# Twenty columns of a V page instead of ten are parked in PSUM between two layers, and one weight piece changes places with a K page

## The chip, the cores and the metric

The kernel runs on one core of one Trainium2 chip. The metric is the device time of one execution in microseconds (us); lower is better.

## The reference

A decoder for one token, two layers with the same weights and the same K and V caches. Cut to what matters:

```python
def _A_ref(x, k_cache, v_cache, wq, wo):          # attention over the last W = 4096 positions
    q = (x @ wq).reshape(1, 1, 32, 192)           # 32 heads of 192
    scores = einsum(q, k_window) * 192 ** -0.5
    o = einsum(softmax(scores), v_window)
    return o.reshape(1, 1, 32 * 192) @ wo

x = x + _A_ref(_layernorm(x), k_cache, v_cache, wq, wo)
x = x + silu_glu(_layernorm(x), w1, w3, w2)       # 640 -> 1536 -> 640
# ... and both lines once more: layer 1 reads the same caches and weights again
```

K and V of the window are 2 x 32 x 4096 x 192 bf16 values, 100.7 MB, read once per layer. Whatever is still on the chip from layer 0 need not be read again in layer 1.

## The kernel before

The heads are worked on in four blocks of eight, each in four "pages" (z = 0 to 3) of K and of V. A page is 64 columns of 192 bf16 values on 128 partitions, 3.1 MB. Nearly all of SBUF is one tile `pg` with seven page slots. All loads go through one plan in a fixed order, and are issued by SP. A load can be issued when everything that was in its place has been read:

```python
def plan(key, at, n, src):
    queue.append((key, at, n, src))

def need(key):
    while key not in place:
        k, at, n, src = queue.pop(0)
        ...
        nc.sync.dma_start(out=pg[:, at:at + n], in_=src)
        place[k] = live[k] = (at, n)
    ...
```

Layer 1 goes through the blocks backwards (3, 2, 1, 0). So the K and V pages of block 3, last used in layer 0, stay in the seven slots over the layer boundary. One V page (block 3, z 0) has no slot. 54 of its 64 columns lie in a separate area, and the other ten wait in PSUM, where DVE puts them with two transposes as 32-bit words and from where it takes them back with two more. The separate area also keeps 12 columns of the page of block 2, z 3:

```python
KEPT_T = 54          # columns of V page (3, 0) kept in SBUF
KEPT_2 = 12          # columns of V page (2, 3) kept in SBUF
PSUM_T = 10          # columns of V page (3, 0) kept in PSUM
...
half = PSUM_T // 2 * DH
held = [t[:, 0:half // 2].bitcast(U32) for t in (aside, s_two[0])]     # two PSUM banks

def hold(x):                                       # end of layer 0
    for i in range(2):
        nc.vector.transpose(held[i], words(x[:, -2 * half:], i))

def put_back():                                    # layer 1, after the first softmax
    key, at = vkeys[1, 3, 0][0], slot(2)
    place[key] = live[key] = (at, 2 * half)
    for i in range(2):
        nc.vector.transpose(words(pg[:, at:at + 2 * half], i), held[i])
```

In layer 1 the page (2, 3) needs only the columns that were not kept:

```python
if (b, z) == (2, 3):
    plan_v(1, b, z, (slot(vs[z]), TP - KEPT_2), (None, KEPT_2))        # 64 - 12 = 52 loaded
```

At the boundary all seven slots are taken. Until layer 1 has used up its first kept K page, only small pieces can be loaded, into rings in the work area: wo, w1, w3, w2 and the wq pieces of layer 1. wq comes in three groups: group 0 (five chunks of 384 KB, columns for block 3), group 1 (five of 768 KB) and group 2 (five of 384 KB). The plan there is:

```python
for g, (c2, n) in enumerate(QGROUPS):
    if g == 2:
        plan_k(1, 2, 0, 1)            # first new K page, into slot 1
    for c in range(NCH):
        o = 4 * QC * c + QC * c2
        plan(("wq", 1, g, c), RING["q"][g][c], QC * n, wq_v[:, o:o + QC * n])
```

`chunks("b3")` in the kernel means group 1, chunk 3; I use the same names: b0 to b4 are group 1, c0 to c4 group 2.

PSUM has eight banks: three fixed tiles (two score tiles and `aside`), three work buffers (`ps_a`) and two small ones (`ps_m`). The Trainium skill, "PSUM — Partial Sum Buffer", section "Specifications (TRN2)", gives 8 banks of 2 KiB per partition. Five columns of 192 bf16 values are 1,920 B, so a bank holds five of them and ten columns fill two banks.

## Time and profile before

| | before |
|---|---|
| median of the first 6 executions | 528.36 us (526.78 to 528.73) |
| span in the profile | 526.9 us (an execution of 528.68 us) |
| bytes over the DMA engines | 219.27 MB, 416 GB/s on average |
| PE / DVE busy | 54% / 48% |
| rate from 20 to 250 us and from 330 to 510 us | 430 and 428 GB/s |
| rate from 270 to 310 us (layer boundary) | 364 to 402 GB/s |

The lines of the page that say so (busy time and share of each engine; then the bytes):

```profile
span 526.9 us, 6780 instructions
PE 282.1 (54%) x2978; PEld 120.1 (23%) x2978; DVE 253.0 (48%) x309; ACT 41.6 (8%) x93; POOL 17.3 (3%) x62
DMA packets 16311, 219.27 MB, mean 416 GB/s; under 512 B 1945, under 2 KB 1945, under 8 KB 7961
```

The table by stretches of time follows: for each stretch (in us from the start) its length, the busy time of each engine, the granted TensorE clock, the busy share of the DMA engines and what they moved.

```profile
core 0: us, PE busy (x) PEld busy (x) DVE busy (x) ACT busy (x) POOL busy (x), PEclk, DMA share, GB/s
20.00:250.00 230.00, 115.79 (x1040) 43.87 (x1036) 129.49 (x125) 15.63 (x36) 0.00 (x0) 0.77 1.01 430
...
270.00:280.00 10.00, 6.23 (x92) 4.11 (x92) 2.10 (x9) 0.79 (x3) 0.00 (x0) 0.50 0.99 381
280.00:290.00 10.00, 6.68 (x109) 5.31 (x102) 1.28 (x6) 0.78 (x3) 2.25 (x7) 0.50 1.01 402
290.00:300.00 10.00, 6.41 (x120) 3.52 (x122) 3.24 (x13) 0.88 (x3) 0.72 (x3) 0.50 1.02 369
300.00:310.00 10.00, 7.70 (x85) 2.99 (x81) 1.34 (x1) 0.48 (x1) 0.00 (x0) 0.84 1.00 364
310.00:320.00 10.00, 6.67 (x108) 2.15 (x101) 2.89 (x12) 1.76 (x4) 2.30 (x6) 0.84 1.01 417
...
330.00:510.00 180.00, 105.11 (x1076) 43.34 (x1072) 97.72 (x100) 12.17 (x28) 0.50 (x2) 0.74 1.00 428
```

The last two columns are the ones to read. In all these stretches the DMA engines are busy all the time (share 0.99 to 1.02). But between 270 and 310 us they move 364 to 402 GB/s and otherwise about 430. So a busy share of 1.00 does not mean full rate.

The issues at the boundary, from the timeline of SP (start, duration, what, how many; neighbours are merged, so the row at 303.48 covers c0 to c4):

```profile
286.43 15.42 SPq L111 DMA_DIRECT2D pg<-in_A_wq_dram  x10
302.88 0.55 SPq L111 DMA_DIRECT2D pg<-in_A_k_cache_dram  x1
303.48 6.11 SPq L111 DMA_DIRECT2D pg<-in_A_wq_dram  x5
309.64 2.86 SPq L111 DMA_DIRECT2D pg<-in_A_k_cache_dram  x2
```

The first new K page is issued at 302.88 us, when PE has read the first kept K page, and c0 right after it. c0's ring place had been read about 8 us earlier. SP issues in order, so the K page holds c0 back.

The transposes into and out of PSUM on DVE, with the idle time before an instruction and what ended it in brackets:

```profile
250.04 0.69 DVE L279 STREAM_TRANSPOSE aside<-pg 128x480 uint32<-128x480 uint32 x1
250.63 0.65 DVE L279 STREAM_TRANSPOSE s_ps_176<-pg 128x480 uint32<-128x480 uint32 x1
...
327.17 0.86 DVE L285 STREAM_TRANSPOSE pg<-aside 128x480 uint32<-128x480 uint32 x1
327.96 0.64 DVE L285 STREAM_TRANSPOSE pg<-s_ps_176 128x480 uint32<-128x480 uint32 x1
330.96 0.17 DVE L425 RECIPROCAL rl<-rl_ps 128x1 f32<-128x1 f32 x1 [2.37 <-PE rl_ps L423]
```

A transpose takes 0.64 to 0.86 us. After the way back DVE waits 2.37 us for the row sums from PE: this is slack. How long SP waited for the second transpose of the way in, from the queue's own waits (total us, times, longest):

```profile
SPq L111 <- DVE s_ps_176 L279: 7.8, 1, 7.8
```

SP waits at this point, but the two V pages that it issued before are still being loaded: their first matmuls wait for data until 257.34 and 264.66 us.

Last, a row of the chain of waits (start, length, what). The chain passes through DVE for 24.7 us after the boundary:

```profile
331.13 24.74 DVE pg L345 x15
```

### The profile page before, as it was taken

The page shows a single profiled execution, that of the slowest core. Times are in us where ns is not written, and L with a number is a line of the kernel's source. Part 1 is how long each engine was busy: PE and PEld are TensorE (multiplying, and loading weights), DVE is VectorE, ACT ScalarE, POOL GpSimd, SP SyncE. Part 2 cuts the span into 40 slices and gives each one's busy share as a digit, 9 for nine tenths or more (in the row PEclk, how much of TensorE's full clock was granted, in tenths as well). Part 3 has the DMA queues.
Part 4 walks back from the last instruction along what each step waited for, and adds up shares of the span by engine and source line. Part 5 has one row for each costly group of instructions (what it writes and reads, how often), then busy time and mean ns, then how long its engine had stood idle before and what let it go on. Part 6 is the DMA issues. An engine that isn't in the chain of part 4 may idle for free.

```text
span 526.9 us, 6780 instructions
## 1 busy us (share of the span) xinstructions
PE 282.1 (54%) x2978; PEld 120.1 (23%) x2978; DVE 253.0 (48%) x309; ACT 41.6 (8%) x93; POOL 17.3 (3%) x62
## 2 busy tenths in 40 slices
PE   1417755550755507647456773694774335844464
PEld 0201111110311103213125321221321121212153
DVE  1269974436394174753001226898475366453010
ACT  0000020000200011002000006001100020002000
POOL 6000000000000000000001004000000000000000
PEclk9997887776589757777555595888687757977555
DMA  8999999999999999999999999999999999999994
GB/s 358 422 442 423 436 422 438 423 435 431 428 430 428 433 425 435 428 421 436 420 403 390 370 374 443 428 431 427 428 430 430 433 429 431 428 428 426 419 409 168
DMA packets 16311, 219.27 MB, mean 416 GB/s; under 512 B 1945, under 2 KB 1945, under 8 KB 7961
## 3 DMA queue, kind: packets, MB, share of 16 engines
q1 hardware_dynamic: 16136, 218.83, 98.3%
q8 instruction: 23, 0.38, 0.3%
q14 instruction: 8, 0.06, 0.0%
q10 hardware_dynamic: 144, 0.00, 0.0%
HBM read 218.83 MB, written 0.00 MB: 415 GB/s over the span
## 4 chain that ended last, share of the span: by engine, by line
DMA 60%; DVE 17%; PE 12%; issue 7%; ACT 3%; SPq 0%; ACTq 0%; DVEq 0%
DMA pg<-in_A_k_cache_dram 39%; DVE pg L345 13%; DMA pg<-in_B_w_dram 7%; DMA pg<-in_A_v_cache_dram 7%; PE s_ps_177 L353 5%; DMA pg<-in_A_wq_dram 5%; PE y_ps L448 2%; PE o_ps L416 2%; PE s_ps_176 L353 2%; DMA xb<-in_A_x_dram 2%; ACT pg L404 2%; ACT pg L391 1%; DVE pg L394 1%; DVE pg L337 1%; DVE otd L440 0%
## 5 line engine op out<-in xcount | busy, mean ns | idle before, releaser
L345 DVE STREAM_TRANSPOSE pg<-pg 128x1536 uint32<-128x1536 uint32 x112 | 188.5, 1743 | 94.2 <-DMA pg<-in_A_k_cache_dram 94.2
L353 PE MATMUL s_ps_176<-pg 128*32 128x512 bf16 x384 | 87.2, 617 | 53.8 <-DVE pg L345 53.8
L353 PE MATMUL s_ps_177<-pg 128*32 128x512 bf16 x288 | 65.7, 616 | 52.1 <-DVE pg L345 49.6
L416 PE MATMUL o_ps<-pg 128*16 128x384 bf16 (+1 forms) x1024 | 74.7, 377 | 27.3 <-DMA pg<-in_A_v_cache_dram 18.9
L353 PEld LDWEIGHTS <-pg 128*32 128x32 bf16 x672 | 41.1, 116 | 202.8 <-issue 190.0
L416 PEld LDWEIGHTS <-pg 128*16 128x16 bf16 (+1 forms) x1024 | 30.8, 98 | 59.2 <-issue 40.1
L433 PE MATMUL ot_ps<-o_sb,pg 128*128 128x192 bf16 x16 | 3.8, 342 | 62.0 <-ACT o_sb L430 62.0
L448 PE MATMUL y_ps<-otd,pg 128*128 128x1 bf16 x540 | 23.3, 178 | 11.4 <-DVE otd L440 6.7
L448 PEld LDWEIGHTS <-pg 128*128 128x128 bf16 x540 | 23.1, 131 | 13.5 <-issue 8.0
L391 ACT ACTIVATE pg<-s_ps_176,pg 32x512 bf16<-32x512 f32 x8 | 6.6, 822 | 185.7 <-DVE pg L388 185.6
L437 DVE SCALAR_TENSOR_TENSOR om<-ot_ps,rl,dsel 128x192 f32<-128x192 f32 x8 | 3.1, 388 | 37.2 <-PE ot_ps L433 37.2
L391 ACT ACTIVATE pg<-s_ps_177,pg 32x512 bf16<-32x512 f32 (+1 forms) x8 | 6.6, 823 | 166.0 <-DVE pg L388 157.5
L404 ACT COPY pg<-pg 32x256 bf16<-32x256 bf16 (+1 forms) x36 | 17.7, 491 | 6.8 <-DVE pg L394 6.2
L394 DVE STREAM_TRANSPOSE pg<-pg 128x1024 bf16<-128x1024 bf16 x8 | 10.0, 1245 | 15.6 <-ACT pg L391 15.6
L232 POOL MEMSET pg<- 128x128 f32 (+1 forms) x6 | 1.4, 240 | 463.6 <-PE u_ps L488 276.7
L433 PEld LDWEIGHTS <-pg 128*128 128x128 bf16 x16 | 1.6, 101 | 65.5 <-issue 65.5
L425 DVE RECIPROCAL rl<-rl_ps 128x1 f32<-128x1 f32 x8 | 1.3, 168 | 29.9 <-PE rl_ps L423 29.8
L317 PE MATMUL q_ps<-pg,xw 128*32 128x384 bf16 x80 | 7.0, 521 | 15.6 <-DVE xw L228 11.1
L317 PEld LDWEIGHTS <-xw 128*32 128x32 bf16 x160 | 5.7, 120 | 33.3 <-issue 20.5
L234 POOL TENSOR_SCALAR_AFFINE_SELECT pg<-pg 128x128 f32<-128x128 f32 (+1 forms) x33 | 12.7, 385 | 2.4 <-POOL pg L232 0.2
L406 DVE COPY pg<-pg 32x256 bf16<-32x256 bf16 (+1 forms) x36 | 11.7, 324 | 0.6
L368 PE MATMUL s_ps_177<-pg 128*32 128x512 bf16 x96 | 11.8, 615 | 0.0
(102 smaller groups left out, 113.1 us busy)
## 6 DMA issues: line engine op xcount, KB each, us to landing
pg<-in_A_k_cache_dram SPq DMA_DIRECT2D x28, 3072.0 KB, 39.8
pg<-in_A_v_cache_dram SPq DMA_DIRECT2D x23, 3072.0 KB, 36.8
pg<-in_A_wo_dram SPq DMA_DIRECT2D x6, 1920.0 KB, 36.3
pg<-in_A_wq_dram SPq DMA_DIRECT2D x2, 3072.0 KB, 16.7
pg<-in_B_w_dram SPq DMA_DIRECT2D x7, 768.0 KB, 6.8
pg<-in_A_v_cache_dram SPq DMA_DIRECT2D x2, 2496.0 KB, 27.3
pg<-in_A_wo_dram SPq DMA_DIRECT2D x6, 640.0 KB, 23.0
pg<-in_A_wq_dram SPq DMA_DIRECT2D x10, 384.0 KB, 11.0
```

What stands on the lines that cost most here:

```text
L234: nc.gpsimd.affine_select(out=t, in_=t, compare_op=ALU.not_equal, fill=1.0, base=base, pattern=pattern, channel_multiplier=1)
L317: nc.tensor.matmul(q_ps[32 * j:32 * j + 32, 0:384], lhsT=xw[:, c, 3 - c2:35 - c2], rhs=w[:, o:o + 384], start=(first and i == 0), stop=(la ...
L345: nc.vector.transpose(v, v)
L353: nc.tensor.matmul(s_ps[64 * h:64 * h + 32, :], lhsT=wst[:, z, h, it, 4 - 4 * th:36 - 4 * th], rhs=_ap(x, 0, P, 192 * th + 64 * be + par + ...
L368: nc.tensor.matmul(s_ps[32 * q:32 * q + 32, :], lhsT=wst[:, z, h, it, 4 - 4 * th:36 - 4 * th], rhs=_ap(x, 0, P, 192 * th + 64 * be + par + ...
L391: nc.scalar.activation(out=_ap(e, 64 * h, rows, h, [[32, 32], [2, 16]]), in_=s_ps[r, :].rearrange("p (t j) -> p t j", j=16), func=ACTF.Exp ...
L394: nc.vector.transpose(et, e)
L404: nc.scalar.copy(out=dst, in_=src)
L406: nc.vector.tensor_copy(out=dst, in_=src)
L416: nc.tensor.matmul(o_ps[32 * j:32 * j + mw, 0:384], lhsT=ptm[:, po:po + mw], rhs=x[:, 384 * i:384 * i + 384], start=st, stop=(last and u > ...
L433: nc.tensor.matmul(ot_ps[:].rearrange("p q i -> p (q i)"), lhsT=csel[:, par, :, :].rearrange("p h q -> p (h q)"), rhs=o_sb[:, 192 * par:19 ...
L448: nc.tensor.matmul(y_ps[:, c:c + 1], lhsT=w[:, D * i + c:D * i + D:NCH], rhs=od[:, ci:ci + 1], start=(first and ci == 0 and c == 0), stop= ...
```

## The change

The intent: park 20 columns instead of ten in PSUM. Then 44 columns of page (3, 0) are enough in SBUF, and the area has room for 22 columns of page (2, 3) instead of 12. In layer 1 the latter loads 42 columns instead of 52. To free two more banks, the work buffers go from three to two, the small ones from two to one; `z_ps` moves into the bank `aside`, and the third query tile is taken later. Besides, the first new K page changes places with c0.

```diff
--- before.py
+++ after.py
@@ -34,9 +34,9 @@
 WST = NZ * 2 * 6 * 36
 AUX = WORK + WST
 KEPT = 14592
-KEPT_T = 54
-KEPT_2 = 12
-PSUM_T = 10
+KEPT_T = 44
+KEPT_2 = 22
+PSUM_T = 20
 SEL = 13504
 KEPT2 = KEPT + KEPT_T * DH
 SLOT0 = KEPT2 + KEPT_2 * DH
@@ -84,8 +84,8 @@
     wrk = ctx.enter_context(tc.tile_pool(name="wrk", bufs=1))
     sml = ctx.enter_context(tc.tile_pool(name="sml", bufs=1))
     ps_s = ctx.enter_context(tc.tile_pool(name="ps_s", bufs=1, space=PSUM))
-    ps_a = ctx.enter_context(tc.tile_pool(name="ps_a", bufs=3, space=PSUM))
-    ps_m = ctx.enter_context(tc.tile_pool(name="ps_m", bufs=2, space=PSUM))
+    ps_a = ctx.enter_context(tc.tile_pool(name="ps_a", bufs=2, space=PSUM))
+    ps_m = ctx.enter_context(tc.tile_pool(name="ps_m", bufs=1, space=PSUM))
     ctx.enter_context(tc.manual_schedule(engines={ENG.SP, ENG.PE, ENG.DVE, ENG.Activation, ENG.Pool}))
 
     pg = pages.tile([P, NPG], BF16, name="pg")
@@ -183,9 +183,9 @@
     plan_cut(("wo", 0, 3), D, CUT_WO, wo_v[3], RING["wo"][0])
     plan_ffn(0, (RING["w1"], RING["w3"], RING["w2"]))
     for g, (c2, n) in enumerate(QGROUPS):
-        if g == 2:
-            plan_k(1, 2, 0, 1)
         for c in range(NCH):
+            if (g, c) == (2, 1):
+                plan_k(1, 2, 0, 1)
             o = 4 * QC * c + QC * c2
             plan(("wq", 1, g, c), RING["q"][g][c], QC * n, wq_v[:, o:o + QC * n])
     plan_v(1, 3, 0, ("psum", PSUM_T), (None, KEPT_T))
@@ -268,21 +268,22 @@
     nc.gpsimd.memset(ls[:], 0.0)
     s_two = [ps_s.tile([P, 512], F32, tag=f"s{i}", name=f"s_ps{i}") for i in range(2)]
     aside = ps_s.tile([P, 512], F32, tag="aside", name="aside")
-    half = PSUM_T // 2 * DH
-    held = [t[:, 0:half // 2].bitcast(U32) for t in (aside, s_two[0])]
+    half = 5 * DH
+    spare = [ps_s.tile([P, 512], F32, tag=f"spare{i}", name=f"spare{i}") for i in range(2)]
+    held = [t[:, 0:half // 2].bitcast(U32) for t in (aside, s_two[0], *spare)]
 
     def words(x, i):
         return x[:, half * i:half * (i + 1)].bitcast(U32)
 
     def hold(x):
-        for i in range(2):
-            nc.vector.transpose(held[i], words(x[:, -2 * half:], i))
+        for i in range(4):
+            nc.vector.transpose(held[i], words(x[:, -4 * half:], i))
 
     def put_back():
         key, at = vkeys[1, 3, 0][0], slot(2)
-        place[key] = live[key] = (at, 2 * half)
-        for i in range(2):
-            nc.vector.transpose(words(pg[:, at:at + 2 * half], i), held[i])
+        place[key] = live[key] = (at, 4 * half)
+        for i in range(4):
+            nc.vector.transpose(words(pg[:, at:at + 4 * half], i), held[i])
 
     wst = pg[:, WORK:WORK + WST].rearrange("p (z h i n) -> p z h i n", z=NZ, h=2, i=6)
     ptm, e, et = pg[:, 0:2048], pg[:, 2048:3072], pg[:, 3072:4096]
@@ -508,7 +509,7 @@
         at = slot(2)
         ident = pg[:, at:at + 2 * P].bitcast(F32)
         selector(ident, [(0, [[-1, P]])])
-        z_ps = ps_a.tile([P, 512], F32, tag="a", name="z_ps")
+        z_ps = aside
         nc.vector.memset(z_ps[:, 0:160], 0.0)
         zr = [z_ps[32 * j:32 * j + 1, 0:160] for j in range(4)]
         for c in range(NCH):
@@ -594,7 +595,7 @@
                 k_ready(order[0], z)
                 k_stage(order[0], z, s_ps, z == 0, z == NZ - 1)
         else:
-            qg = [ps_a.tile([P, 512], F32, tag="a", name=f"qg_ps{g}") for g in range(3)]
+            qg = [ps_a.tile([P, 512], F32, tag="a", name=f"qg_ps{g}") for g in range(2)]
             q_mms(qg[0], 0, (0,))
             st, rstd = statistics()
             q_mms(qg[0], 0, range(1, NCH))
@@ -628,6 +629,7 @@
             softmax_back()
         else:
             softmax_front(s_ps, l, 64)
+            qg.append(ps_a.tile([P, 512], F32, tag="a", name="qg_ps2"))
             chunks("c0", "c1", "c2", "c3", "c4")
             qproj_tail(qg[2], *QGROUPS[2], rstd)
             softmax_back(True)
```

The Trainium skill, "VectorE: DVE Perf Modes", section "The three transpose paths", says that DVE transposes in blocks of 32 x 32 only. Here that does no harm, as the same operation on the way back undoes it; the results of every run below passed the comparison (a weak check, as e4 will show).

## The prediction

> What bounds the kernel now. The page gives a span of 526.9 us, 219.27 MB over the DMA engines, 416 GB/s on average. The table by 10 us windows shows the DMA engines about 100% busy from 10 to 510 us, mostly at 425 to 434 GB/s, except at the layer boundary (260 to 320 us: 410, 381, 402, 369, 364, 417). PE is busy 54%, DVE 48%. A K page takes 39.8 us from issue to landing, while 3.1 MB need 7.3 us at 430 GB/s, so several pages are queued outside the boundary. The kernel is bound by bytes, plus what a shallow queue loses at the boundary. The Trainium skill, "DMA: Bandwidth & Descriptors", section "Where 436 GB/s comes from", derives a ceiling of 435.2 GB/s; the plateau agrees.
>
> Removed: in layer 1 the V page of block 2, z 3, is loaded with 42 columns instead of 52; ten columns are 128 x 10 x 192 x 2 B = 491,520 B, at 430 GB/s 1.14 us (estimate). Layer 0 loads the same bytes, cut differently.
>
> Added: two more DVE transposes 128x480 into PSUM (now 0.69 and 0.65 us, at 250 us) and two more out of it (0.86 and 0.64 us, at 327 us): about 1.3 us of DVE each time.
> - Going in: the issue of the last V page of layer 0, now at 251.4 us, waits for the second transpose, so it and the wo pieces move 1.3 us later. But the two V pages ahead of it land at 257.3 and 264.6 us, so the queue is not empty: cost 0.
> - Coming back: after the second transpose ends at 328.6 us, DVE waits for the row sums until 330.96 us. The 1.3 us fit in that gap: cost 0 to 0.2 us.
>
> Moved: the first new K page is issued at 302.88 us, when the PE has read the kept page in its slot; the wq piece behind it goes at 303.48 us although its ring place has been free since about 295 us. After: the wq piece goes at about 301.9 us, the K page still at 302.9 us. The pieces before land at 305.8 and 308.4 us, 2.6 to 3.3 us apart for 786 KB, where 1.8 us is usual; 304 to 308 us move 340 GB/s. 0.39 MB more in the queue should win back 0.2 to 0.5 us. The K page's transposes start only at 331 us, so its later place costs nothing.
>
> PSUM: work tiles go from three buffers to two, small ones from two to one. The order on PE stays. The new waits (y after the read of ot, row sums after the read of the earlier y) are on things long done or already required through the data: cost 0.
>
> All of the saved transfer is on the path: DMA is saturated from the reduced page to 510 us. Predicted: 528.36 - 1.14 - 0.3 = 526.9 us; 8 in 10 between 525.6 and 528.2. Faster by over 2%: 0.01; within 2%: 0.98; slower: 0.01.
>
> Right if: DMA bytes fall to 218.78 MB; the plateau stays at 428 to 434; 300 to 310 us moves more than 364 GB/s; the last w2 piece lands 1 to 2 us earlier; after the return from PSUM DVE still waits for the row sums and the K transposes start near 331 us.
>
> Wrong if: the longer hold starves the queue at 250 to 275 us; the K transposes start over 1 us later and late slot releases make the queue run dry in 340 to 400 us; the single small PSUM buffer stretches the feed-forward chain at 274 to 292 us; or the moved wq piece only delays the pieces ahead of it.

## More of the kernel before

In the long stretches the kernel is bound by bytes; at the boundary something is lost besides.

What is lost there can be seen in part in the trace's records of single DMA packets, which no view prints. From 20 to 250 us most bytes move in packets of 24,576 B, which take 0.913 us in the median; sixteen engines at that pace would move 431 GB/s (worked out from the two numbers). From 270 to 310 us most bytes move in packets of 3,072, 5,120 and 6,144 B, which take 0.121, 0.196 and 0.234 us in the median; the same sum gives 406, 418 and 420 GB/s. So a part of the loss goes with the smaller packets. The rest lies in packets that took far longer: those of 6,144 B took 0.264 us on average and up to 1.79 us. Why, the trace does not tell.

## The result

| | before | after |
|---|---|---|
| median | 527.84 us (20 executions) | 526.11 us (10 executions) |
| range | 526.78 to 528.99 us | 525.80 to 527.40 us |
| ratio | | 0.9970, 95% interval 0.9961 to 0.9979 |
| span in the profile | 526.9 us | 524.0 us |
| bytes | 219.27 MB | 218.78 MB |

Ratios are computed as the mean time of one kernel's runs over that of the other's of the same rounds, so a ratio is not quite that of the medians quoted. Here the means differ by 1.57 us (527.94 and 526.37).

The two profiles differ by 2.9 us, nearly twice as much. The profile of before was taken on an execution of 528.68 us, slower than its median, and that of after on one of 525.75 us, faster than any of the ten timed ones. A difference of two profiles is here as uncertain as what is being looked for. The times decide, and the profiles are read for rates, bytes and order.

The page of after, the same lines:

```profile
span 524.0 us, 6786 instructions
PE 283.0 (54%) x2978; PEld 119.9 (23%) x2978; DVE 255.3 (49%) x313; ACT 41.6 (8%) x93; POOL 17.1 (3%) x62
DMA packets 16310, 218.78 MB, mean 417 GB/s; under 512 B 1944, under 2 KB 1944, under 8 KB 7832
```

0.49 MB fewer, and 2.3 us more of DVE work, which four more transposes, 0.56 us apart, account for (2.2 us). The same stretches, with the same columns:

```profile
20.00:250.00 230.00, 115.41 (x1036) 43.33 (x1028) 129.46 (x124) 15.67 (x36) 0.00 (x0) 0.74 1.01 430
270.00:280.00 10.00, 6.14 (x88) 3.97 (x91) 1.97 (x9) 0.65 (x2) 0.00 (x0) 0.50 0.97 368
300.00:310.00 10.00, 7.69 (x88) 2.75 (x84) 1.34 (x1) 0.48 (x1) 0.00 (x0) 0.95 1.03 390
310.00:320.00 10.00, 6.25 (x104) 2.11 (x97) 3.11 (x12) 1.74 (x4) 4.35 (x12) 0.90 1.02 422
330.00:510.00 180.00, 108.14 (x1086) 44.71 (x1083) 98.18 (x103) 12.22 (x29) 0.50 (x2) 0.73 1.00 428
```

The rate in the long stretches is the same, 430 and 428 GB/s. From 300 to 310 us it is 390 instead of 364, but a second profile of the same kernel (e0) has only 376. Stretches of 10 us at the boundary scatter by that much from execution to execution. From 270 to 280 us it is 368 instead of 381. The change moves no load there, but the last V page before it goes out 1.3 us later (below). The five profiled kernels with ten columns in PSUM have 375 to 381 GB/s in this stretch, the eight with twenty 364 to 376 (without e5), so this may be a real cost of the longer way in; the means differ by 7 GB/s, 0.07 MB in 10 us, which is less than 0.2 us (an estimate). The issues:

```profile
286.53 16.47 SPq L111 DMA_DIRECT2D pg<-in_A_wq_dram  x11
303.05 0.55 SPq L111 DMA_DIRECT2D pg<-in_A_k_cache_dram  x1
306.58 2.69 SPq L111 DMA_DIRECT2D pg<-in_A_wq_dram  x4
```

c0 has moved into the first row (11 pieces), four are left after the K page. The timeline of SP, narrowed to c0 itself:

```profile
301.64 1.36 SPq L111 DMA_DIRECT2D pg<-in_A_wq_dram  x1
```

c0's issue starts at 301.64 us, as predicted, but lasts 1.36 us where the median of wq pieces is 0.33 us, and ends at 303.00 us. The K page follows at 303.05 us. So the head start of c0 over the K page was shorter in this execution than the plan suggests. In e0, the same kernel, c0's issue took 0.42 us:

```profile
302.30 0.42 SPq L111 DMA_DIRECT2D pg<-in_A_wq_dram  x1
```

So the long issue is an accident of one execution and no property of the change. The Trainium skill, "Perfetto Trace Analysis", section "DMA Instruction — HWDGE (DVE, Sync)", says that this window covers the issue (lock, descriptor generation, semaphore), not the movement of data. What held the one of 1.36 us up is not in the trace.

The transposes on DVE:

```profile
250.26 0.69 DVE L280 STREAM_TRANSPOSE aside<-pg 128x480 uint32<-128x480 uint32 x1
...
251.97 0.65 DVE L280 STREAM_TRANSPOSE spare_180<-pg 128x480 uint32<-128x480 uint32 x1
...
326.53 0.87 DVE L286 STREAM_TRANSPOSE pg<-aside 128x480 uint32<-128x480 uint32 x1
327.32 0.64 DVE L286 STREAM_TRANSPOSE pg<-s_ps_176 128x480 uint32<-128x480 uint32 x1
327.88 0.65 DVE L286 STREAM_TRANSPOSE pg<-spare_179 128x480 uint32<-128x480 uint32 x1
328.44 0.65 DVE L286 STREAM_TRANSPOSE pg<-spare_180 128x480 uint32<-128x480 uint32 x1
330.71 0.17 DVE L426 RECIPROCAL rl<-rl_ps 128x1 f32<-128x1 f32 x1 [1.62 <-PE rl_ps L424]
330.80 1.76 DVE L346 STREAM_TRANSPOSE pg<-pg 128x1536 uint32<-128x1536 uint32 x1
```

On the way in there are four instead of two, 0.56 us apart. On the way back DVE still waits 1.62 us for the row sums, and the K transposes start at 330.80 us, as before (331.05). SP's wait for the transposes into PSUM:

```profile
SPq L111 <- DVE spare_180 L280: 9.2, 1, 9.2
```

It grew from 7.8 to 9.2 us, and the last V page of layer 0 is issued at 252.70 instead of 251.36 us. The first w1 piece, behind that page's three pieces and three of wo, is issued at 257.42 us against 257.32 before. Both times a V page lands at that moment (its matmuls start at 257.45 and 257.34 us). SP's own waits from 255 to 258 us, before and after, name it:

```profile
SPq L111 <- DMA pg<-in_A_v_cache_dram: 1.9, 1, 1.9
SPq L111 <- DMA pg<-in_A_v_cache_dram: 0.8, 1, 0.8
```

So the piece waits for this page in any case, 1.9 us before and 0.8 us after; the delay has vanished by then.

### The profile page after: what moved, and what is told of

It is laid out like the page before. It is cut to its first block, busy times and chain, and to the rows that moved or that the text cites. A ratio compares the mean times of both kernels' runs of the same rounds, so it can differ in the third digit from the quotient of the medians.

```text
span 524.0 us, 6786 instructions
## 1 busy us (share of the span) xinstructions
PE 283.0 (54%) x2978; PEld 119.9 (23%) x2978; DVE 255.3 (49%) x313; ACT 41.6 (8%) x93; POOL 17.1 (3%) x62
## 2 busy tenths in 40 slices
DMA packets 16310, 218.78 MB, mean 417 GB/s; under 512 B 1944, under 2 KB 1944, under 8 KB 7832
## 4 chain that ended last, share of the span: by engine, by line
DMA 60%; DVE 17%; PE 13%; issue 7%; ACT 3%; SPq 0%; ACTq 0%; DVEq 0%
DMA pg<-in_A_k_cache_dram 39%; DVE pg L346 13%; DMA pg<-in_B_w_dram 7%; DMA pg<-in_A_v_cache_dram 7%; PE s_ps_177 L354 5%; DMA pg<-in_A_wq_dram 5%; PE o_ps L417 2%; PE y_ps L449 2%; PE s_ps_176 L354 2%; DMA xb<-in_A_x_dram 2%; ACT pg L405 2%; ACT pg L392 1%; DVE pg L395 1%; DVE pg L338 1%; DVE otd L441 0%
## 5 line engine op out<-in xcount | busy, mean ns | idle before, releaser
L417 PE MATMUL o_ps<-pg 128*16 128x384 bf16 (+1 forms) x1024 | 77.5, 388 | 27.4 <-DMA pg<-in_A_v_cache_dram 18.8
```

What stands on the lines that cost most here:

```text
L417: nc.tensor.matmul(o_ps[32 * j:32 * j + mw, 0:384], lhsT=ptm[:, po:po + mw], rhs=x[:, 384 * i:384 * i + 384], start=st, stop=(last and u > ...
```

## The experiments

The theory (the sum): 10 columns are 0.49 MB, 1.14 us at 430 GB/s, all of it on the path; the moved wq piece gives a little (0.2 to 0.5 us); transposes and smaller pools cost nothing. The rivals: the order gives most; or DVE, which the chain of waits names after the boundary, sets the pace; or smaller pools cost something that a larger gain hides. There were twelve runs of eleven kernels (e0 is the changed kernel, e1 ran twice); all passed the comparison with the reference. Each was compared with runs of the kernel before on the same chip. For e4 to e7 these are the nine executions of an earlier job and a single new one (527.85 us), so a drift of the chip between the two jobs is hardly checked. The means in the table are plain means; the recorded ratios weigh the executions a little differently.

| run | what | median us | mean against before | ratio, 95% interval |
|---|---|---|---|---|
| e0 | the changed kernel again | 526.40 | -1.34 us | 0.9974 (0.9962 to 0.9987) |
| e1 | order alone | 527.57 | -0.27 | 0.9994 (0.9982 to 1.0007) |
| e1b | order alone, again | 526.89 | -0.75 | 0.9984 (0.9971 to 0.9997) |
| e2 | all but the order | 526.36 | -1.32 | 0.9975 (0.9962 to 0.9987) |
| e3 | smaller pools alone | 528.07 | +0.56 | 1.0010 (0.9996 to 1.0024) |
| e4 | 40 more columns not loaded | 521.93 | -5.74 | 0.9887 (0.9871 to 0.9902) |
| e5 | way in five times | 527.95 | +0.33 | 1.0010 (0.9997 to 1.0022) |
| e6 | way back three times | 526.51 | -1.06 | 0.9980 (0.9966 to 0.9994) |
| e7 | c0 before b3 | 525.56 | -2.31 | 0.9956 (0.9943 to 0.9970) |
| e8 | c0 before b2 | 525.28 | -2.40 | 0.9955 (0.9943 to 0.9967) |
| e9 | K page behind two pieces | 526.52 | -1.17 | 0.9978 (0.9963 to 0.9993) |
| e10 | e7's order, nothing else | 527.69 | -0.20 | 0.9997 (0.9980 to 1.0014) |

### e0: the yardstick

No edit. Expected:

> The changed kernel again, on the same chip as the next three, as their yardstick. Both theories: 1.4 to 1.7 us faster than before (ratio 0.9968 to 0.9974), since 10 columns fewer take 1.14 us at 430 GB/s and the earlier wq piece is believed to give the rest.

Measured: 1.34 us faster than before; the interval holds the 1.57 us of the first comparison.

### e1 and e1b: the order alone

```diff
 for g, (c2, n) in enumerate(QGROUPS):
-    if g == 2:
-        plan_k(1, 2, 0, 1)
     for c in range(NCH):
+        if (g, c) == (2, 1):
+            plan_k(1, 2, 0, 1)
```

> Only the plan's order is changed: one wq piece before the first new K page; columns and PSUM as before. Sum theory (bytes and order add up): 0.2 to 0.6 us faster than before, ratio about 0.9992, and 300 to 310 us move more than 364 GB/s, about 390. Rival (bytes alone): ratio 1.000, no more data moved there in the end. Rival (order alone makes the gain): 1.4 us or more faster, 0.9973.

Measured: 0.27 us faster; the interval holds both the theory and no effect. 300 to 310 us moved 382 GB/s. As this did not decide, it was run once more:

> e1 once more, since its interval (0.9982 to 1.0007) held both the theory (0.9992) and no effect. Both runs together should halve that doubt: theory 0.2 to 0.6 us faster, rival 0.

Measured: 0.75 us faster, outside the expectation's 0.6 on the high side. The ten executions of both runs together are 0.52 us faster than those of before, with a standard error of 0.17 us, as worked out from the single executions. So the order alone is very likely worth something in the kernel before, about half a microsecond (the interval of e1b leaves out a ratio of 1, that of e1 holds it), and it is not the main part.

### e2: all but the order

The changed kernel with e1's edit undone (the K page planned before c0 again).

> The whole change except the plan's order, which is as before. Sum theory: 1.0 to 1.3 us faster than before (ratio 0.9978), and 300 to 310 us move about 364 GB/s again. Bytes alone: as fast as the changed kernel, 1.5 us. Order alone: no faster than before.

Measured: 1.32 us faster than before, 0.02 us from e0 on the same chip. So columns and PSUM without the order give the change's gain within the noise. The interval is about 0.65 us to either side, so 0.2 or 0.5 us for the order is not excluded. From 300 to 310 us 374 GB/s were moved, against 376 in e0: no difference to see.

### e3: smaller pools alone

```diff
-ps_a = ctx.enter_context(tc.tile_pool(name="ps_a", bufs=3, space=PSUM))
-ps_m = ctx.enter_context(tc.tile_pool(name="ps_m", bufs=2, space=PSUM))
+ps_a = ctx.enter_context(tc.tile_pool(name="ps_a", bufs=2, space=PSUM))
+ps_m = ctx.enter_context(tc.tile_pool(name="ps_m", bufs=1, space=PSUM))
...
-    z_ps = ps_a.tile([P, 512], F32, tag="a", name="z_ps")
+    z_ps = aside
...
-    qg = [... for g in range(3)]
+    qg = [... for g in range(2)]
...
     softmax_front(s_ps, l, 64)
+    qg.append(ps_a.tile([P, 512], F32, tag="a", name="qg_ps2"))
```

> Only the PSUM pools shrink (two work buffers, one small buffer, z in the bank kept aside, third query group's tile taken later); columns and order as before. Theory: ratio 1.000 within 0.0005, since the new waits are on things long done. Rival (a hidden cost of the smaller pools, made good by a larger gain elsewhere): 0.3 us or more slower.

Measured: 0.56 us slower, with an interval from 0.2 us faster to 1.3 us slower. It doesn't exclude zero, and it doesn't exclude the rival. The mean is outside what the theory allowed (0.0005 is 0.26 us); its standard error is 0.21 us. The trace doesn't show the cost where the prediction would have it: the feed-forward chain, from the first matmul of `ot_ps` to the first of wq, runs from 273.45 to 292.37 us here and from 273.55 to 292.38 us in before. The K transposes start at 332.27 instead of 331.05 us, 1.2 us later, but going by e6, where 2.7 us of delay cost 0.3 us, this would be about 0.1 us (an estimate). See the discussion.

### e4: forty more columns are not loaded

A wrong result: 40 columns of the page are whatever was in the slot. (It passed the comparison all the same, so the comparison does not see so small a part of the attention. That is no proof of correctness for this page.)

```diff
-            nc.sync.dma_start(out=pg[:, at:at + n], in_=src)
+            if k == ("v", 1, 2, 3, 0):
+                nc.sync.dma_start(out=pg[:, at:at + 2 * DH], in_=kv_src(A_v_cache, 2, 3, 0, 2))
+            else:
+                nc.sync.dma_start(out=pg[:, at:at + n], in_=src)
```

> Wrong result on purpose: the changed kernel, but the reduced V page of layer 1 loads only its first 2 columns instead of 42; everything else, PE and DVE work too, stays. 40 columns are 1.966 MB. Theory (every byte taken from that page is on the path): 4.6 us faster than the changed kernel, 6.0 us faster than before (ratio 0.9886). Rival (DVE and PE set the pace after the boundary, as the chain of waits has it there): less than 2.5 us faster than the changed kernel, ratio above 0.9925.

Measured: ratio 0.9887, where 0.9886 was expected. Against e0, which ran on the same chip in another job, 40 columns are worth 5.74 - 1.34 = 4.4 us (standard error 0.4 us; 4.6 us by the recorded ratios), 0.11 us per column; 4.6 us were predicted. (That the means of before are alike, 527.65 and 527.67, is no evidence that the jobs are: they share nine of their ten executions.) Nothing else was changed; PE and DVE did all of their work. So the bytes of this page are on the path, and DVE is not the pace. Ten columns are then worth 1.1 us (4.4 / 4, standard error 0.1 us) if the gain is the same for each column, as the bytes are.

### e5: the way into PSUM five times

```diff
 def hold(x):
-    for i in range(4):
-        nc.vector.transpose(held[i], words(x[:, -4 * half:], i))
+    for i in range(20):
+        nc.vector.transpose(held[i % 4], words(x[:, -4 * half:], i % 4))
```

> The changed kernel with each transpose into PSUM done five times: 16 more of 0.56 us, about 9 us of DVE, before the last V page of layer 0 may be issued. Theory (two V pages are queued until 264.8 us, so the queue does not run dry): issue moves from 252.7 to about 261.7 us, cost 0 to 0.5 us against the changed kernel (ratio to before 0.997 to 0.998). Rival (the hold is on the path): 4 to 9 us slower, ratio above 1.005.

Measured: 0.33 us slower than before, so 1.7 us slower than e0. The expectation of at most 0.5 us was a miss, and so was the rival's 4 to 9 us. The stretches of e5 show it:

```profile
260.00:270.00 10.00, 3.61 (x44) 1.57 (x47) 1.71 (x4) 0.00 (x0) 0.00 (x0) 0.67 0.82 300
270.00:280.00 10.00, 6.36 (x92) 3.95 (x85) 1.47 (x6) 0.48 (x1) 0.00 (x0) 0.50 1.02 419
```

From 260 to 270 us only 300 GB/s are moved, with a share of 0.82: here the queue did run dry. The last V page went out at 261.73 us, as expected. When did the queue run dry? One microsecond, 262 to 263 us, of e0 and then of e5:

```profile
262.00:263.00 1.00, 0.00 (x0) 0.00 (x0) 0.00 (x0) 0.00 (x0) 0.00 (x0) 0.50 0.76 320
262.00:263.00 1.00, 0.00 (x0) 0.00 (x0) 0.00 (x0) 0.00 (x0) 0.00 (x0) 1.00 0.06 25
```

In e5 the share falls from 0.97 (259 to 260 us) over 0.80 and 0.57 to these 0.06: the bytes of the two V pages ahead are moved by then, although the first matmuls on the second of them start at 264.54 us only. The late page was issued when the queue was already running out, and its first packet moved at 263.06 us, 1.3 us after its issue (packet records; in e0 at 261.02 us). The theory had counted the pages ahead up to the first matmul on them (264.66 us), and that is some 4 us more than they keep the engines busy. The wo and w1 pieces behind are late too (the first w1 piece at 265.29 instead of 257.70 us in e0), which leaves less in the queue. Part of the loss comes back from 270 to 280 us (419 GB/s against 364 in e0). The way in thus has slack, but it ends somewhere between the change's own 1.3 us, which move the first w1 piece by 0.1 us, and 9 us.

### e6: the way back three times

```diff
-    for i in range(4):
-        nc.vector.transpose(words(pg[:, at:at + 4 * half], i), held[i])
+    for i in range(12):
+        nc.vector.transpose(words(pg[:, at:at + 4 * half], i % 4), held[i % 4])
```

> The changed kernel with each transpose out of PSUM done three times: 8 more of 0.56 us, 4.5 us of DVE, of which about 1.6 us fall into DVE's wait for the row sums; the K transposes start about 2.9 us later. Theory (pages are queued deep enough): cost 0 to 0.5 us, ratio to before 0.997 to 0.998. Rival (DVE is the pace from 331 to 364 us, as the chain of waits says): about 2.9 us slower than the changed kernel, ratio about 1.003.

Measured: 0.28 us slower than e0 (-1.06 against -1.34 us, standard error 0.35 us). The timeline of DVE in e6:

```profile
326.94 0.87 DVE L286 STREAM_TRANSPOSE pg<-aside 128x480 uint32<-128x480 uint32 x1
...
332.80 1.21 DVE L286 STREAM_TRANSPOSE pg<-spare 128x480 uint32<-128x480 uint32 x2
333.93 0.14 DVE L426 RECIPROCAL rl<-rl_ps 128x1 f32<-128x1 f32 x1
333.99 1.75 DVE L346 STREAM_TRANSPOSE pg<-pg 128x1536 uint32<-128x1536 uint32 x1
```

The wait for the row sums is gone, and the K transposes start at 333.99 us, 2.7 us later than in e0 (331.33). The kernel pays a tenth of that, within the noise. The chain of waits led through 24.7 us of DVE here, and yet DVE can be 2.7 us later for almost nothing: from 330 to 510 us 427 GB/s are moved, against 428 in e0.

### e7 and e8: c0 further ahead

```diff
+        if (g, c) == (1, 3):                      # e7; (1, 2) in e8
+            plan(("wq", 1, 2, 0), RING["q"][2][0], QC, wq_v[:, 0:QC])
+        if (g, c) == (2, 0):
+            continue
```

This is on top of the changed kernel.

> The changed kernel with the same wq piece (third group, chunk 0) two places further ahead, before chunk 3 of the second group: it can be issued at about 298 us, when its ring place has been free since 295 us. If a fuller queue at 296 to 304 us is worth anything: 0.2 to 0.6 us faster than the changed kernel, ratio to before about 0.9965, and 290 to 310 us move more. If the boundary's rate is not set by the number of pieces queued: no difference (0.9973), or slower, because the piece delays the two that the scores wait for.

> As e7, but the piece one place further ahead still, before chunk 2 of the second group; it can be issued at about 295.2 us, the moment its ring place is free. If the queue is as shallow at 295 to 298 us as later: another 0 to 0.4 us faster than e7 (525.56), ratio to before about 0.9950. Rival (the piece now delays chunks 2 and 3, whose scores release the first K slots): 0.3 us or more slower than e7.

Measured: 2.31 and 2.40 us faster than before, about 1.0 us faster than e0 (standard error 0.3 us), more than the 0.2 to 0.6 us that were expected of e7. e7 is by its mean faster than both kernels. e8 is no better than e7, and the prediction that another 0 to 0.4 us may come is neither confirmed nor refuted. Two rows of e7's stretches:

```profile
290.00:300.00 10.00, 6.18 (x114) 3.38 (x116) 3.26 (x13) 0.88 (x3) 0.52 (x2) 0.50 0.99 363
300.00:310.00 10.00, 7.15 (x84) 2.66 (x80) 1.34 (x1) 0.48 (x1) 0.00 (x0) 0.95 1.04 412
```

From 300 to 310 us it moves 412 GB/s, the most of any run here. But that doesn't explain the gain: from 290 to 310 us e7 moves 387 GB/s on average and e8, which is as fast, only 375, where e0 moves 376. The cause stays open. e7's intervals to before and e0's overlap slightly (0.9943 to 0.9970 and 0.9962 to 0.9987), but e8 came to the same value on another chip.

### e9: the K page behind two pieces

```diff
-        if (g, c) == (2, 1):
+        if (g, c) == (2, 2):
             plan_k(1, 2, 0, 1)
```

> The changed kernel with the first new K page behind two wq pieces instead of one. The second of them needs the ring place of chunk 3 of the second group, so the K page's issue moves from about 303 to about 306.7 us, and only one or two wq pieces are queued in between. Theory (the number of bytes queued sets the rate at the boundary): 0.5 to 2 us slower than the changed kernel, ratio to before 0.9983 to 1.001. Rival (order does not matter): 0.9973.

Measured: 1.17 us faster than before, so by the means 0.2 to 0.4 us slower than the changed kernel (its two means: -1.34 and -1.57), with a standard error of 0.4 us. The expectation, at least 0.5 us, was not met by the means, but is not excluded. The K page did go out later, at 307.18 us, and the queue did run low:

```profile
300.00:310.00 10.00, 7.43 (x80) 3.11 (x79) 1.34 (x1) 0.48 (x1) 0.00 (x0) 0.73 0.88 322
310.00:320.00 10.00, 5.81 (x104) 2.83 (x97) 2.65 (x11) 1.72 (x4) 3.92 (x11) 0.96 1.02 429
```

300 to 310 us moved 322 GB/s, share 0.88. Against the changed kernel's 390 these are 0.68 MB fewer, 1.6 us at 430 GB/s (an estimate), which the mean time does not show. The profiled execution of e9 took 527.18 us, 0.6 us more than its mean. Where the rest was made good is not known. (Nor is a low rate there a mark of this order: e4, with the changed kernel's own order, moved 336 GB/s from 300 to 310 us, share 0.96.)

### e10: e7's order in the kernel before

e7's plan with columns and PSUM as before.

> The kernel before with e7's order alone: the wq piece goes before chunk 3 of the second group, columns and PSUM as before. If order and columns add up: 0.8 to 1.2 us faster than before, ratio about 0.998. If e7's gain needs the change's other parts: no faster than e1, 0.9994 to 1.000.

Measured: 0.20 us faster, with executions from 526.07 to 529.25 us, the widest scatter of all. The interval (0.9980 to 1.0014, 1.1 us faster to 0.7 us slower) holds both the theory and its rival. This run decides nothing. Taken with e1b, which does less and came out faster, it shows that the value of an order at the boundary cannot be told to better than some half microsecond with five or six executions.

## Why the prediction was right

- Time. Predicted 526.9 us from 528.36, a gain of 1.44 us, in a range of 525.6 to 528.2. Measured: 526.11 us, a gain of 1.57 us by the means. Of the 0.8 us between predicted and measured time, 0.5 us come from the start: 20 executions of before have a median of 527.84 us, not the 528.36 of the first six. The predicted range holds even this 527.84, so that the time lies in it proves little; the interval of the ratio, which lies wholly below 1, says more. That the sum of the terms comes within 0.2 us of the measured gain is in part luck, as its term for the order (0.3 us) is not settled.
- The bytes. Predicted 218.78 MB, plateau unchanged, 1.14 us. The bytes and the plateau (430 and 428 GB/s) are as predicted, and e4 gives 1.1 us for ten columns. This is shown. It is also the main part: e2, without the order, has all of the gain within its interval.
- The way in costs 0. The w1 piece behind is not delayed by the change (257.42 against 257.32 us). The reason given, two V pages ahead, was right in kind but mis-sized: in e5 these pages keep the engines busy until about 260 us, not 264.6, and the slack ends somewhere between 1.3 and 9 us. A cost below 0.2 us (the rate from 270 to 280 us) is not excluded.
- The way back costs 0 to 0.2 us. DVE still waits for the row sums after the change, and even 2.7 us of delay cost about 0.3 us (e6).
- The order is worth 0.2 to 0.5 us. Not settled. e1 and e1b together say 0.52 us (standard error 0.17) without the columns, e0 against e2 says 0.02 us with them. The predicted rate from 300 to 310 us (over 364 GB/s) was met, 390 in one execution and 376 in another, but e2, without the order, reached 374, and e4, with it, only 336. Such a stretch is no evidence. Nor is it shown that a shallow queue causes the low rate at the boundary: the share stays near 1.00 there, and smaller and some long packets are seen in the records.
- The smaller pools cost 0. Not shown. e3 gave +0.56 us with zero inside its interval, and its trace doesn't show where it would lose it. Against a cost of that size speaks that e2, which has the same pools, gained 1.32 us where e4's slope gives 1.1 us for its columns, so that nothing is missing. That is an argument from a sum with an uncertainty of about 0.6 us, not a measurement.
- The last w2 piece lands 1 to 2 us earlier. Its matmuls start at 520.04 instead of 522.93 us, 2.9 us earlier. The check was badly chosen: it compares two single profiles, which differ by more than the effect.

Left open: whether order and columns add up, why e9 paid so little, where e7's gain comes from, and what the smaller pools cost. They would need several times as many executions of each kernel.

## What to carry to other kernels

In a stretch in which the DMA engines are busy all the time, bytes taken off a load can be worth their time at the plateau rate: here 1.97 MB taken off one page were worth 4.4 us, where 430 GB/s give 4.6 (shown for this page alone). Work added to another engine can cost next to nothing as long as it ends before someone waits for it. Loads that are ahead in the queue cover a delay only until their last bytes are moved, not until their first use (e5). The chain of waits can lead through an engine that has slack; delay that engine on purpose to see if it counts. For effects below the scatter of an execution, measure a larger dose (40 columns instead of ten) rather than the change itself, and don't read terms out of two single profiles.

## What the Trainium skill lacked or had wrong

- "DMA: Bandwidth & Descriptors", section "Where 436 GB/s comes from": it derives 435.2 GB/s, and the plateau of 430 and 428 GB/s over long stretches agrees. The same section says that for HBM to SBUF the HBM side, about 358 GB/s, binds. Where one core alone is in use, it did not: loads from HBM ran at 430 GB/s from 20 to 250 us. The page's section "Measured (HBM→SBUF, 128 partitions, SWDGE, issued from GpSimd)" has 425 GB/s for a core whose neighbour is idle, and keeps about 358 for both cores at once; only the sentence by itself is wrong.
- The same page has rates by size for loads through GpSimd, but none measured on this chip for packets of 3 to 24 KB with many loads in flight. Here the median packets of 3,072, 5,120, 6,144 and 24,576 B give 406, 418, 420 and 431 GB/s for 16 engines (worked out from their durations). At the layer boundary the four stretches of 10 us from 270 to 310 us moved 362 to 410 GB/s in the changed kernel, with a DMA share of 0.97 to 1.03: the busy share does not show the loss.
- "Perfetto Trace Analysis", section "DMA Instruction — HWDGE (DVE, Sync)", tells what the issue's window covers, but gives no durations: the issue of one of the 15 wq pieces of layer 1 took 0.33 us in the median and 1.34 us at most before; c0's took 1.36 us after and 0.42 us in e0.
- "VectorE: DVE Perf Modes", section "The three transpose paths", lists only SBUF as the target of the DVE transpose. Here it writes PSUM and reads PSUM with 32-bit words: 128x480 took 0.65 to 0.69 us into PSUM and 0.64 to 0.65 us out of it (0.86 or 0.87 us for the first), 0.56 us apart back to back.
